# First MLP stage of the next block ahead of the second stage of this one: retention and an exact-GELU MLP on one core

## The chip, the cores and the metric

The kernel runs on one core of one Trainium2 chip. The metric is the device time of one execution in microseconds. The kernel before takes 281.17 us, the median of three runs (280.98 to 282.06).

## The reference

```python
# q, k, v: (8, 8, 576, 64) float32     batch, heads, sequence, head width
scores = (1 / sqrt(64)) * q @ k.T
gamma  = 1 - 2 ** (-5 - arange(8))               # one per head
Dmat   = where(rel >= 0, gamma ** rel, 0)        # rel = row - column
ret    = (scores * Dmat) @ v                     # retention, no softmax
x      = ret.transpose(0, 2, 1, 3).reshape(4608, 512)
h      = x @ w_in                                # (512, 2048)
g      = 0.5 * h * (1 + erf(h / sqrt(2)))        # exact GELU
out    = g @ w_out                               # (2048, 512), float32
```

## The kernel before

The 4608 tokens are cut into nine blocks of 512 (t = 0 to 8). A block goes through three parts.

**Retention** makes the transposed block xT (512 features on partitions in four chunks, 512 tokens). It works on units of 128 tokens: q, k and v are loaded with a cast to bf16 by GpSimd's DMA queue (L522, the 64-token tails of a sequence L518) into a ring of N_LD buffer pairs (qk_ld, v_ld), a pair of units to a buffer. The first ten units are transposed by TensorE (qk_ps, copied to qkT), later ones by DMA transposes that SyncE issues (L613). Then come the scores (sc), the masked scores (ret, VectorE), the scaled values (vh, VectorE L826 or eight pieces on ScalarE L829), the product of the two and of the running state (o_ps), the state itself (u_ps, copied to u_sb), and the scaling into xT (VectorE L860, L848). The rings of vh, ret and qkT have N_VH, N_RET and N_QKT buffers. The matmuls of retention come in bursts between MLP products; a burst can carry the last products of one group of units and the scores of the next together, and the numbers in APART name the groups whose scores stand by themselves.

**The first stage** multiplies xT by w_in and applies GELU, which gives g. Blocks 0 and 1 do it plainly (hT, ScalarE L1104). From block 2 on the hidden features are cut into four parts, kp = 0 to 3, and a part is done either plainly (four tiles of hT, 16 matmuls of 512 columns) or as a "unit" of seven products instead of eight quarter products (four matmuls of 256 columns each, into PSUM tiles yT, zT and xT_, in the order of PRODUCTS). A unit needs sums of xT (xs, VectorE L1059), sums of w_in (wi_sum) and a chain behind each product: copies m3 ('q') and raw ('t') of yT on VectorE or ScalarE (L573, L575), then on VectorE less (L1196), more (L1200), dif (L1209) and c11 (L1226), and four GELUs on ScalarE (L1217). LAYOUTS says for each block which parts are units, which are plain ("p") and which are woven.

**The second stage** multiplies g by w_out. Block 0 does it plainly; from block 1 on it is seven products of 16 matmuls of 256 columns for each half of rows (oT, in the order of SECOND), with sums of g (s, g, VectorE L1004) and of w_out, and with chains on ScalarE and VectorE (L1235, L1238, L1243, L1248, L1254) into o_sb, two tiles with one buffer each, that SyncE stores (L1306).

The order of all instructions is made when the kernel is built, by a planner in the kernel: each step is added with an engine, a duration, its dependencies and a due time (add), and a loop places the step that can start first, with ties broken by due times. For TensorE the MLP products come from `stream`, a list of runs: before, the first stage of block t and the second stage of block t, for t = 0 to 8. pe_candidates looks at the first LOOK products of the foremost run that still has some (for blocks 0 and 1 also of later runs). Each engine then executes its list in order and waits at semaphores. The same holds for the DMA queues: ORDER is the list of the loads up to unit 10 and of the weights (k2 is k of unit 2, wi4 the fifth eighth of w_in, L528, wo0 the first of w_out, L531), and GpSimd issues them in that order; SyncE's list has the transposes and the stores.

g has one buffer for each half of the parts (tags g0 and g1), so that a block's first stage can write g when the second stage of the block ahead has read it.

Of the kernel before, what the change touches and what calls it, by code (L numbers as in the profile page):

```python
# [9 lines left out]
FP32 = mybir.dt.float32  # L10
BF16 = mybir.dt.bfloat16
# [96 lines left out]
def kernel(  # L108
# [12 lines left out]
    B, H, S, D = q.shape  # L121
# [8 lines left out]
    TOK = 512  # L130
    HALF = TOK // 2
    N_BLK = n_tok // TOK
# [16 lines left out]
    kept = pair_of[1, 0]  # L149
# [11 lines left out]
    def slot_of(i):  # L161
# [4 lines left out]
    v_order[n:n] = kept  # L166

    N_PE_TR = 10
    N_LD = 4
    N_QKT = 4  # L170
    N_VH = 5
    N_RET = 3
    N_Q = 4
    VH_ACT = [6, 8, 10, 11, 12, 13, 14, 15, 16, 17, 19, 21, 22, 24, 27, 28, 31, 34, 35, 37]
    HOT = 10.1
    N_WARM = 8
    SLACK = 0.2
    CUTS = (0, 128, 256, 384, 512)
    AHEAD = 6
    WIDE = [2, 6, 14, 10, 4]  # L180
    VH_DUE = 14.0
    PARTS = 4
    FAST = 1
    FETCH = 4.0
    BUSY_FETCH = 6.2
    GAP_A = 0.0
    GAP_B = 1.3
    SHIFT = {4: -1.5, 5: -11.5, 6: 1.0, 7: 3.0, 8: 4.0, 9: -1.5, 10: 1.0, 11: 1.0, 12: 1.5, 13: -3.0, 14: -1.0, 15: -0.5, 16: -5.0, 17: -4.5, 18: -1.5, 19: 3.5, 20: 6.5}
    APART = [6, 7, 12]
    BEFORE = 6.1  # L190
    UNIT_FROM = 2
    LOOK = 16
    HOLD = 5.6
    LAYOUTS = {2: ['10', '2', 'p3'], 3: ['01', '2', 'p3'], 4: ['1', '02', 'p3'], 5: ['01', '2', 'p3'], 6: ['01', '23'], 7: ['01', '23'], 8: ['10', '3p2']}
    LEAD = 8.9
    SPREAD = 7.7
    EASE = 6.8
    ORDER = ("k2 wi4 q1 q2 k3 pos k1 wi0 q3 v1 v3 v2 wi3 wi6 wi1 wi7 v4 q4 wi5 k5 wi2 k4 q5 v5 wo0 wo4 wo1 wo5 q9 "
             "k7 k6 wo6 q6 q8 v10 q7 wo2 v6 wo7 v9 wo3 k10 q10 v7 k8 k9 v8").split()
    K_ORDER = [0, 1, 8, 9, 2, 3, 10, 11, 4, 5, 12, 13, 6, 7, 14, 15]  # L200
    PRODUCTS = "3251647"
    SECOND = "1267543"
    LAYOUT = {t: ["p0", "p1", "p2", "p3"] for t in range(2, N_BLK)}
    for t in range(UNIT_FROM, N_BLK):
# [2 lines left out]
    const = ctx.enter_context(tc.tile_pool(name="const", bufs=1))  # L207
    ld_pool = ctx.enter_context(tc.tile_pool(name="ld", bufs=N_LD))
    tr_pool = ctx.enter_context(tc.tile_pool(name="tr", bufs=N_QKT))
    f_pool = ctx.enter_context(tc.tile_pool(name="fold", bufs=2))  # L210
# [4 lines left out]
    g_pool = ctx.enter_context(tc.tile_pool(name="g", bufs=1))  # L215
# [4 lines left out]
    P = Plan()  # L220
# [57 lines left out]

    ld_ring, tr_ring, vh_ring, ret_ring, x_ring = Ring(N_LD), Ring(N_QKT), Ring(N_VH), Ring(N_RET), Ring(3)
    o_ring = [Ring(1), Ring(1)]  # L280
    g_ring = [Ring(1) for _ in range(2)]
    s_ring = [Ring(1) for _ in range(2)]
    f_ring, m_ring, xs_ring = Ring(2), Ring(N_Q), Ring(1)

# [1 line left out]
    def laid(t, block):  # L286


        def plain_of(kp):
            return [("1", t, m, 1, 0, TOK) for m in (2 * kp, 2 * kp + 1, 2 * kp + 8, 2 * kp + 9)]  # L290

        def unit_of(kp):
            return [("u", t, kp, p) for p in PRODUCTS]

        if block[0] == "p":
            return plain_of(int(block[1]))
        one = unit_of(int(block[0]))
        if len(block) == 1:
            return one
        if block[1] == "p":  # L300
            four = plain_of(int(block[2]))
            return [one[0], four[0], one[1], one[2], four[1], one[3], four[2], one[4], one[5], four[3], one[6]]
        return [x for two in zip(one, unit_of(int(block[1]))) for x in two]

    stream = []
    for t in range(N_BLK):
        if t < 2:
            cuts = CUTS if t == 0 else (0, 256, 512)
            for lo, hi in zip(cuts, cuts[1:]):
                stream.append([("1", t, m, 2, lo, hi) for m in K_ORDER[::2] if t or m not in WIDE])  # L310
            if t == 0:
                stream.append([("1", t, m + n, 1, 0, TOK) for m in WIDE for n in range(2)])
        else:
            stream.append([one for block in LAYOUT[t] for one in laid(t, block)])
        if t < FAST:
            stream.append([("2", t, ts, m, m + 2) for m in range(0, N_DF, 2) for ts in range(2)])
            stream.append([("2", t, ts, m, m + 4) for ts in range(2, 4) for m in range(0, N_DF, 4)])
        else:
            stream.append([("2", t, p, r, n, part) for n, p in enumerate(SECOND) for r in ((0, 1), (1, 0))[t == N_BLK - 1]
                           for part in range(2)])  # L320

    def piece_time(one):
        if one[0] == "u":
# [20 lines left out]
    first = {}  # L344
    for nm, src, eng, tag in (("q", q, nc.sync, "t"), ("k", k, nc.scalar, "t"), ("v", v, nc.sync, "o0")):
        t = first[nm] = (o_pool if nm == "v" else f_pool).tile([128, H, D], FP32, tag=tag, name=f"{nm}32")
# [7 lines left out]
    lgT = const.tile([128, HP, 1], FP32, name="lgT")  # L354
    step = const.tile([128, HP, 1], FP32, name="step")
    back_step = const.tile([128, HP, 1], FP32, name="back_step")
    val = const.tile([128, 1, 128], FP32, name="val")
    pos = const.tile([128, 1, NCI], FP32, name="pos")
    far = const.tile([128, 1, 128], FP32, name="far")
    ident = const.tile([128, 1, 128], BF16, name="ident")  # L360
    near = const.tile([128, HP, 2, 128], FP32, name="near")
    msk = const.tile([128, 1, 128], FP32, name="msk")
# [113 lines left out]

    loaded, slots, w_in_sb, w_out_sb = {}, {}, {}, {}
    touched = {}

    def tiles_of(i):  # L480

        if i not in loaded:
            n = slot_of(i)
            if i in kept:
                loaded[i] = (const.tile([128, 2, H, D], BF16, name=f"qk_ld{i}"), const.tile([128, H, D], BF16, name=f"v_ld{i}"))
                return loaded[i]
            if n not in slots:
                ld_ring.take()
                slots[n] = (ld_pool.tile([128, 2, H, 2, D], BF16, tag="qk", name="qk_ld"),
                            ld_pool.tile([128, 2, H, D], BF16, tag="v", name="v_ld"))  # L490
            qk, v_ld = slots[n]
            j = units[i][2] or 0
            if i in old:
                loaded[i] = (qk.rearrange("p a (j h) b d -> p j a (h b) d", j=2)[:, j], v_ld[:, j])
            else:
                loaded[i] = (qk[:, :, :, j], v_ld[:, j])
        return loaded[i]
# [45 lines left out]
    for item in ORDER:  # L543
        what = item.rstrip("0123456789")
        i = int(item[len(what):] or 0)
# [334 lines left out]
    for i in range(N_U):  # L880
        bp, ci, j = units[i]
# [4 lines left out]
        if i < N_PE_TR:  # L886
            for jj, nm in enumerate("qk"):
# [3 lines left out]
                    lambda engine, i=i, jj=jj: turned_copy(i, jj, engine), due - 1.0)  # L891
# [3 lines left out]
        if i not in fine and i not in tails:  # L895
# [8 lines left out]
            if ci:  # L904
# [4 lines left out]
                at=lambda i=i: 0.0 if i // 4 in x_tiles else x_ring.at())  # L909
# [16 lines left out]
        else:  # L926
            add(f"mask{n}.1", "dve", 0.6, (last if n in ALONE else [f"odd_{n}"]) + ["msk"], lambda n=n: masked(n, 1), due + 2.0,
                at=ret_ring.at)
# [4 lines left out]
    for i in v_order:  # L933
# [4 lines left out]
        if i in VH_ACT:  # L938
            step_ = H // PARTS
            for p in range(PARTS):  # L940
                name = f"vh{i}" if p == PARTS - 1 else f"vh{i}.{p}"
# [33 lines left out]
    g_tiles, s_tiles, w_sums, fold = {}, {}, {}, {}  # L975
# [9 lines left out]
    def g_of(t, m):  # L985
        kp = m % 8 // 2
        two = kp // 2
        if (t, two) not in g_tiles:
            if t:
                g_ring[two].take()  # L990
            g_tiles[t, two] = g_pool.tile([128, 2, 2, 2, TOK], BF16, tag=f"g{two}" if t else f"first{two}", name="g")
        return g_tiles[t, two][:, kp % 2]

    def g_sum(t, two, which):
# [327 lines left out]
    for run in stream:  # L1322
        for one in run:
            nm = f"mlp{one}"
            if one[0] == "1":
                _, t, m0, n, lo, hi = one
# [210 lines left out]
    def begun(one):  # L1537
# [7 lines left out]
            return one[2] in "12" or (one[2] in OPENS and one[3] == rs[0]) or BANK2[one[2]] in chain.get(("2", one[1], rs), ())  # L1545
        return True

    def pe_candidates():
        got = []
        for op in P.open["pe"]:  # L1550
            if op.name in in_macro or op.name.startswith("mlp"):
                continue
            got.append((max(T["pe"], op.ready, nth_free(op.banks)), 0, op.due, op))
        window = 0
        hold = False
        if macros and not got:
            ahead = next((W[r[0]] for r in heads if r), NEVER)
            n, ops, due = macros[0]
            hold = ahead >= due + HOLD and (macro_start(ops, False) or NEVER) <= T["pe"] + 0.3
        for run in heads:  # L1560
            if not run:
                continue
            if run[0][1] < 2:
                look = run[:1]
            else:
                look = run[:LOOK]
            for one in look:
                op = P.ops[f"mlp{one}"]
                if not op.waits and not (hold and op.banks) and begun(one):
                    got.append((max(T["pe"], op.ready, nth_free(op.banks)), 2, W[one], op))  # L1570
            window += 1
            if window >= (AHEAD if run[0][1] < 2 else 1):
                break
        got = [g for g in got if g[0] < NEVER / 2]
        if macros and not any(g[1] == 0 for g in got):
            n, ops, due = macros[0]
            at = macro_start(ops)
            if at is not None:
                at = max(at, stretch_end[0] + (GAP_B if ops[0].startswith("in_b") else GAP_A))
                ahead = next((W[r[0]] for r in heads if r), NEVER)  # L1580
                mlp = min((g[0] for g in got if g[1] == 2), default=NEVER)
                if ahead >= due or mlp > T["pe"] + 0.4:
                    got.append((at, 1, due, ops))
        if not got:
            return None
        first = min(g[0] for g in got)
        return min((g for g in got if g[0] <= first + 0.05), key=lambda g: (g[1], g[2], g[0]))
# [76 lines left out]
```

## Time and profile before

| what | value |
|---|---|
| median of three runs | 281.17 us (280.98 to 282.06) |
| the profiled execution | 281.36 us, its span 279.5 us |
| TensorE busy (PE) | 271.7 us, 97% of the span |
| VectorE busy (DVE) | 229.8 us, 82% |
| ScalarE busy (ACT) | 176.2 us, 63% |
| GpSimd busy (POOL) | 110.2 us, 39%, nearly all DMA issues |
| granted TensorE clock | 1.00 |
| units of seven products in the first stages | 23 of 28 parts |
| last matmul group ends | at 276.3 us |

PE is the matmul side of TensorE and PEld its weight loads, which overlap with it. Busy time says how long an engine had an instruction under way. The profile's waits say for whom an engine sat idle. A place in the text such as "at 121.7" is microseconds from the start of the span.

### The profile page before, as it was taken

Reading aid. Unit: us, or ns where it says so; the run is one execution under the profiler, and the core shown is the slowest. Engines: PE = TensorE matmul, PEld = TensorE weight load, DVE = VectorE, ACT = ScalarE, POOL = GpSimd, SP = SyncE. Lnnn points to the kernel's source line nnn. Section 1 sums busy time; section 2 is a strip of 40 time slices with the busy share of each in tenths; the row PEclk is TensorE's granted clock in tenths of the full one; section 3 lists DMA queues with packets and bytes.
Section 4 is the critical chain, followed back from the end, with each engine's and each line's share of the span. In section 5 each row is a group of like instructions: output and inputs, shape, how many; then the busy total and the mean of one; then the engine's idle time right before and its main releaser. Section 6 shows DMA issues by size and latency. Waiting matters only on the chain.

```text
span 279.5 us, 8688 instructions
## 1 busy us (share of the span) xinstructions
PE 271.7 (97%) x3607; PEld 215.7 (77%) x3623; DVE 229.8 (82%) x440; ACT 176.2 (63%) x434; POOL 110.2 (39%) x139
## 2 busy tenths in 40 slices
PE   7899999999999999999999999999999999999995
PEld 2584566578888688858886888778888888888784
DVE  5950757499999997899989999988799989958841
ACT  7586425567839974795189625982695379618741
POOL 8967869847546067710526448305000000000000
PEclk9999999999999999999999999999999999999999
DMA  9999999999999999999999999999700040013013
GB/s 154 165 187 172 191 169 178 136 231 144 131 131 138 214 114 142 145 198 166 130 220 115 118 139 243 145 112 94 196 2 2 6 150 4 2 38 115 0 40 113
DMA packets 152374, 35.55 MB, mean 127 GB/s; under 512 B 141072, under 2 KB 148240, under 8 KB 152336
## 3 DMA queue, kind: packets, MB, share of 16 engines
q0 software_dynamic: 115792, 17.97, 101.3%
q1 hardware_dynamic: 34912, 16.26, 34.3%
q10 hardware_dynamic: 1632, 0.79, 1.1%
q8 instruction: 28, 0.46, 0.7%
q14 instruction: 10, 0.08, 0.1%
HBM read 36.70 MB, written 9.44 MB: 165 GB/s over the span
## 4 chain that ended last, share of the span: by engine, by line
PE 78%; DMA 11%; POOL 7%; issue 1%; ACT 1%; DVE 0%; POOLq 0%; ACTq 0%
PE oT L231 37%; PE zT L231 11%; PE hT L231 8%; PE yT L231 7%; DMA qk_ld<-in_k_dram 5%; PE o_ps L231 4%; DMA qk_ld<-in_q_dram 3%; DMA w_in<-in_moe_w_in_dram 3%; POOL qk_ld L522 3%; PE sc L231 2%; PE u_ps L231 2%; POOL v_ld L522 2%; POOL qk_ld L518 1%; POOL w_in L528 1%; ACT g L1217 0%
## 5 line engine op out<-in xcount | busy, mean ns | idle before, releaser
L231 PEld LDWEIGHTS <-g 128*128 128x128 bf16 x576 | 55.0, 98 | 13.1 <-DVE g L1004 0.3
L231 PEld LDWEIGHTS <-w_in 128*128 128x128 bf16 x528 | 47.2, 98 | 15.8 <-issue 0.2
L231 PEld LDWEIGHTS <-wi_sum 128*128 128x128 bf16 x460 | 44.6, 98 | 7.8 <-issue 0.9
L231 PE MATMUL hT<-xT,w_in 128*128 128x256 bf16 (+2 forms) x334 | 49.7, 292 | 0.6
L1104 ACT ACTIVATE g<-hT 128x512 bf16<-128x512 f32 (+1 forms) x58 | 32.1, 555 | 23.4 <-PE hT L231 22.6
L231 PE MATMUL oT<-w_out,g 128*128 128x256 bf16 (+1 forms) x315 | 45.4, 293 | 0.3 <-issue 0.2
L829 ACT ACTIVATE vh<-v_ld,dv 128x64 bf16<-128x64 bf16 x152 | 41.8, 345 | 1.4 <-DVE qkT L573 1.3
L1248 ACT COPY o_sb<-oT 128x512 f32<-128x512 f32 (+1 forms) x27 | 14.5, 539 | 42.2 <-PE oT L231 35.2
L231 PEld LDWEIGHTS <-s 128*128 128x128 bf16 x384 | 37.1, 98 | 4.7
L522 POOL DMA_DIRECT2D qk_ld<-in_q_dram x31 | 27.7, 896 | 31.5 <-DMA qkT<-qk_ld 23.7
L522 POOL DMA_DIRECT2D v_ld<-in_v_dram x31 | 27.9, 903 | 14.6 <-issue 5.0
L231 PE MATMUL oT<-w_sum,s 128*128 128x256 bf16 x256 | 31.8, 273 | 0.0
L231 PE MATMUL oT<-w_sum,g 128*128 128x256 bf16 x256 | 31.3, 273 | 0.0
L522 POOL DMA_DIRECT2D qk_ld<-in_k_dram x31 | 28.0, 903 | 5.8 <-DMA v_ld<-in_v_dram 5.2
L1217 ACT ACTIVATE g<-zT 128x512 bf16<-128x512 f32 x46 | 26.2, 605 | 2.2 <-PE zT L231 1.5
L657 DVE TENSOR_TENSOR ret<-sc,msk 128x512 bf16<-128x512 f32 x36 | 23.1, 680 | 0.5 <-PE sc L231 0.5
L860 DVE TENSOR_TENSOR xT<-o_ps,dqT 128x512 bf16<-128x512 f32 x26 | 16.7, 680 | 0.6 <-PE o_ps L231 0.6
L826 DVE TENSOR_TENSOR vh<-v_ld,dv 128x512 bf16<-128x512 bf16 x17 | 11.5, 683 | 6.6 <-DMA v_ld<-in_v_dram 6.6
L573 DVE COPY qkT<-qk_ps 128x512 bf16<-128x512 bf16 x17 | 6.7, 420 | 12.3 <-PE qk_ps L235 12.3
L1196 DVE TENSOR_TENSOR q<-q,zT 128x512 f32<-128x512 f32 x23 | 14.9, 681 | 2.1 <-PE zT L231 1.9
L1254 DVE TENSOR_TENSOR o_sb<-o_sb,oT 128x512 f32<-128x512 f32 (+1 forms) x18 | 11.2, 622 | 6.4 <-PE oT L231 4.0
L1226 DVE TENSOR_TENSOR zT<-q,zT 128x512 f32<-128x512 f32 x23 | 15.6, 690 | 1.0 <-PE zT L231 0.6
(174 smaller groups left out, 461.2 us busy)
## 6 DMA issues: line engine op xcount, KB each, us to landing
out_dram<-o_sb SPq DMA_DIRECT2D x29, 256.0 KB, 3.4
qk_ld<-in_k_dram POOLq DMA_DIRECT2D x31, 128.0 KB, 8.0
qk_ld<-in_q_dram POOLq DMA_DIRECT2D x31, 128.0 KB, 8.0
v_ld<-in_v_dram POOLq DMA_DIRECT2D x31, 128.0 KB, 7.6
w_in<-in_moe_w_in_dram POOLq DMA_DIRECT2D x8, 256.0 KB, 8.0
w_out<-in_moe_w_out_dram POOLq DMA_DIRECT2D x8, 256.0 KB, 7.9
out_dram<-o_sb SPq DMA_DIRECT2D x9, 128.0 KB, 2.4
v_ld<-in_v_dram POOLq DMA_DIRECT2D x8, 64.0 KB, 6.3
```

The lines of the kernel that those rows point to most:

```text
L231: return nc.tensor.matmul(*args, **more)
L522: nc.gpsimd.dma_start(dst, src[2 * bp + j, :, ci * C:ci * C + C, :].rearrange("h s d -> s h d"))
L657: nc.vector.tensor_tensor(r, t, by, op=ALU.mult)
L826: nc.vector.tensor_tensor(vh, loaded[i][1], dv[:, :, ci:ci + 1].to_broadcast([128, H, D]), op=ALU.mult)
L829: nc.scalar.activation(vh[:, h], loaded[i][1][:, h], AF.Copy, scale=dv[:, h, ci:ci + 1])
L860: nc.vector.tensor_tensor(dst, o, dqT[:, :, ci * C:ci * C + C], op=ALU.mult)
L1104: nc.scalar.activation(g_of(t, m0)[:, m0 % 2:m0 % 2 + n, m0 // 8, lo:hi], hT, AF.Gelu)
L1196: nc.vector.tensor_tensor(q_, q_, chain[key]["Z"][1], op=ALU.subtract)
L1217: nc.scalar.activation(target(key, what), chain[key][n][1], AF.Gelu)
L1226: nc.vector.tensor_tensor(to, chain[key]["q"], z, op=ALU.add)
L1248: nc.scalar.copy(target(key, what), chain[key][n][1])
L1254: nc.vector.tensor_tensor(to, to, chain[key][n][1], op=ALU.add)
```

## The change

The order of the runs in `stream` changes. With LAG = 4 the first stage of block 4 comes right behind that of block 3, and from there on the first stage of a block stands ahead of the second stage of the block before: F3, F4, S3, F5, S4, F6, S5, F7, S6, F8, S7, S8. So g of two blocks is alive: blocks 2, 4, 6 and 8 get buffers of their own (tag "again"). Space for them comes from smaller rings (load buffers 4 to 3, vh 5 to 4, ret 3 to 2) and from sharing: the loads of the units in `kept` lie in the first "again" buffer, and two start-up tiles in a q tile. When 13 products or fewer of the foremost run are left (EDGE), TensorE may also take products of the next run. The planner's numbers are searched anew: the order of loads, the layouts, which units have their vh on ScalarE (20 before, 17 after), due times and gaps.

```diff
-    N_LD = 4
+    N_LD = 3
-    N_VH = 5
-    N_RET = 3
+    N_VH = 4
+    N_RET = 2
-    VH_ACT = [6, 8, 10, 11, 12, 13, 14, 15, 16, 17, 19, 21, 22, 24, 27, 28, 31, 34, 35, 37]
+    VH_ACT = [4, 6, 7, 8, 9, 13, 14, 16, 18, 19, 22, 24, 28, 30, 31, 32, 36]
+    EDGE = 13
-    WIDE = [2, 6, 14, 10, 4]
+    WIDE = [2, 10, 14, 12, 4]
...
-    APART = [6, 7, 12]
-    BEFORE = 6.1
+    APART = [6, 7, 8, 9, 10, 11]
+    BEFORE = 9.9
-    LOOK = 16
-    HOLD = 5.6
-    LAYOUTS = {2: ['10', '2', 'p3'], 3: ['01', '2', 'p3'], 4: ['1', '02', 'p3'], 5: ['01', '2', 'p3'], 6: ['01', '23'], 7: ['01', '23'], 8: ['10', '3p2']}
+    LAG = 4
+    LOOK = 11
+    HOLD = 6
+    LAYOUTS = {2: ['0', '12', 'p3'], 3: ['01', '2', 'p3'], 4: ['3', '2', '0p1'], 5: ['10', '23'], 6: ['01', '2p3'], 7: ['01', '23'], 8: ['01', '2', '3']}
-    ORDER = ("k2 wi4 q1 q2 k3 pos k1 wi0 q3 v1 v3 v2 wi3 wi6 wi1 wi7 v4 q4 wi5 k5 wi2 k4 q5 v5 wo0 wo4 wo1 wo5 q9 "
-             "k7 k6 wo6 q6 q8 v10 q7 wo2 v6 wo7 v9 wo3 k10 q10 v7 k8 k9 v8").split()
+    ORDER = ("k2 k1 pos q1 wi0 q3 k3 q2 v1 v2 v3 wi4 wi7 wi1 wi5 v4 k4 q5 wi6 k5 wi3 wi2 q4 wo0 v5 wo4 wo1 q9 wo5 "
+             "q8 v7 wo6 v6 q7 q6 wo2 k7 v10 wo7 wo3 k6 q10 k8 v8 k10 k9 v9").split()
-    PRODUCTS = "3251647"
+    PRODUCTS = "3251467"
...
-    g_ring = [Ring(1) for _ in range(2)]
+    g_ring = [Ring(2) for _ in range(2)]
...
+    stream = []
+    for t in range(N_BLK):
+        first_stage(t)
+        if t != LAG - 1:
+            second_stage(t - (t >= LAG))
+    second_stage(N_BLK - 1)
...
-            g_tiles[t, two] = g_pool.tile([128, 2, 2, 2, TOK], BF16, tag=f"g{two}" if t else f"first{two}", name="g")
+            g_tiles[t, two] = g_pool.tile([128, 2, 2, 2, TOK], BF16, tag=f"first{two}" if not t else f"g{two}" if t % 2 else f"again{two}", name="g")
...
+    def ending(run):
+
+        return run[0][1] > 1 and len(run) <= EDGE and not any(P.ops[f"mlp{one}"].banks for one in run) and run is heads_left()[0]
...
-            if window >= (AHEAD if run[0][1] < 2 else 1):
+            if window >= (AHEAD if run[0][1] < 2 else 1) and not ending(run):
                 break
```

The other edits are the due times SHIFT, LEAD, SPREAD and EASE, the gaps GAP_A, GAP_B and SLACK, and the sharing of space.

More of the change, by code (lines that the diff above doesn't have):

```diff
@@ L168 @@
     N_PE_TR = 10
-    N_LD = 4
+    N_LD = 3
     N_QKT = 4
-    N_VH = 5
-    N_RET = 3
+    N_VH = 4
+    N_RET = 2
     N_Q = 4
-    VH_ACT = [6, 8, 10, 11, 12, 13, 14, 15, 16, 17, 19, 21, 22, 24, 27, 28, 31, 34, 35, 37]
+    VH_ACT = [4, 6, 7, 8, 9, 13, 14, 16, 18, 19, 22, 24, 28, 30, 31, 32, 36]
     HOT = 10.1
     N_WARM = 8
-    SLACK = 0.2
+    SLACK = 0.1
+    EDGE = 13
     CUTS = (0, 128, 256, 384, 512)
     AHEAD = 6
-    WIDE = [2, 6, 14, 10, 4]
+    WIDE = [2, 10, 14, 12, 4]
     VH_DUE = 14.0
@@ L185 @@
     BUSY_FETCH = 6.2
-    GAP_A = 0.0
-    GAP_B = 1.3
-    SHIFT = {4: -1.5, 5: -11.5, 6: 1.0, 7: 3.0, 8: 4.0, 9: -1.5, 10: 1.0, 11: 1.0, 12: 1.5, 13: -3.0, 14: -1.0, 15: -0.5, 16: -5.0, 17: -4.5, 18: -1.5, 19: 3.5, 20: 6.5}
-    APART = [6, 7, 12]
-    BEFORE = 6.1
-    UNIT_FROM = 2
-    LOOK = 16
-    HOLD = 5.6
-    LAYOUTS = {2: ['10', '2', 'p3'], 3: ['01', '2', 'p3'], 4: ['1', '02', 'p3'], 5: ['01', '2', 'p3'], 6: ['01', '23'], 7: ['01', '23'], 8: ['10', '3p2']}
-    LEAD = 8.9
-    SPREAD = 7.7
-    EASE = 6.8
-    ORDER = ("k2 wi4 q1 q2 k3 pos k1 wi0 q3 v1 v3 v2 wi3 wi6 wi1 wi7 v4 q4 wi5 k5 wi2 k4 q5 v5 wo0 wo4 wo1 wo5 q9 "
-             "k7 k6 wo6 q6 q8 v10 q7 wo2 v6 wo7 v9 wo3 k10 q10 v7 k8 k9 v8").split()
+    GAP_A = 1.7
+    GAP_B = 2.4
+    SHIFT = {4: 1.5, 5: 6.5, 6: 8.5, 7: 1.0, 8: 6.5, 9: 1.5, 10: 0.0, 11: -3.5, 12: -6.0, 13: -6.5, 14: -4.5, 15: -4.0, 16: -0.5, 17: 0.5, 18: -2.0, 19: -2.0, 20: 2.0}
+    APART = [6, 7, 8, 9, 10, 11]
+    BEFORE = 9.9
+    UNIT_FROM = 2
+    LAG = 4
+    LOOK = 11
+    HOLD = 6
+    LAYOUTS = {2: ['0', '12', 'p3'], 3: ['01', '2', 'p3'], 4: ['3', '2', '0p1'], 5: ['10', '23'], 6: ['01', '2p3'], 7: ['01', '23'], 8: ['01', '2', '3']}
+    LEAD = 8
+    SPREAD = 7.5
+    EASE = 4.6
+    ORDER = ("k2 k1 pos q1 wi0 q3 k3 q2 v1 v2 v3 wi4 wi7 wi1 wi5 v4 k4 q5 wi6 k5 wi3 wi2 q4 wo0 v5 wo4 wo1 q9 wo5 "
+             "q8 v7 wo6 v6 q7 q6 wo2 k7 v10 wo7 wo3 k6 q10 k8 v8 k10 k9 v9").split()
     K_ORDER = [0, 1, 8, 9, 2, 3, 10, 11, 4, 5, 12, 13, 6, 7, 14, 15]
-    PRODUCTS = "3251647"
+    PRODUCTS = "3251467"
     SECOND = "1267543"
@@ L303, in laid, with first_stage @@
         return [x for two in zip(one, unit_of(int(block[1]))) for x in two]
-    stream = []
-    for t in range(N_BLK):
+    def first_stage(t):
         if t < 2:
@@ L314, with second_stage @@
             stream.append([one for block in LAYOUT[t] for one in laid(t, block)])
+    def second_stage(t):
         if t < FAST:
@@ L356 @@
     back_step = const.tile([128, HP, 1], FP32, name="back_step")
-    val = const.tile([128, 1, 128], FP32, name="val")
+    start_up = f_pool.tile([128, 2, HALF], FP32, tag="q", name="start_up", bufs=N_Q)
+    val, far = start_up[:, 0:1, :128], start_up[:, 1:2, :128]
     pos = const.tile([128, 1, NCI], FP32, name="pos")
-    far = const.tile([128, 1, 128], FP32, name="far")
     ident = const.tile([128, 1, 128], BF16, name="ident")
@@ L478 @@
     touched = {}
+    early = []
     def tiles_of(i):
@@ L484, in tiles_of @@
             if i in kept:
-                loaded[i] = (const.tile([128, 2, H, D], BF16, name=f"qk_ld{i}"), const.tile([128, H, D], BF16, name=f"v_ld{i}"))
+                if not early:
+                    early.append(g_pool.tile([128, 2, 2, 2, TOK], BF16, tag="again0", name="qkv_ld").rearrange("p a b h s -> p (a b h s)"))
+                at = 3 * H * D * kept.index(i)
+                loaded[i] = (early[0][:, at:at + 2 * H * D].rearrange("p (j h d) -> p j h d", j=2, h=H),
+                             early[0][:, at + 2 * H * D:at + 3 * H * D].rearrange("p (h d) -> p h d", h=H))
                 return loaded[i]
@@ L1546, in begun, with heads_left @@
         return True
+    def ending(run):
+        return run[0][1] > 1 and len(run) <= EDGE and not any(P.ops[f"mlp{one}"].banks for one in run) and run is heads_left()[0]
+    def heads_left():
+        return [run for run in heads if run]
     def pe_candidates():
```

## The prediction

> **What bounds the kernel now.** I read the page's busy shares first, then the waits of PE, the windows by stage and the timeline of the first 18 us.
>
> From the page:
>
> ```profile
> span 279.5 us, 8688 instructions
> PE 271.7 (97%) x3607; PEld 215.7 (77%) x3623; DVE 229.8 (82%) x440; ACT 176.2 (63%) x434; POOL 110.2 (39%) x139
> qk_ld<-in_k_dram POOLq DMA_DIRECT2D x31, 128.0 KB, 8.0
> ```
>
> All of PE's own waits, and three windows of 28 to 30 us (columns: length, PE, PEld, DVE, ACT, POOL, then clock and DMA):
>
> ```profile
> PE warm L231 <- DVE ln_scale L352: 1.2, 1, 1.2
> PE qk_ps L235 <- DMA qk_ld<-in_q_dram: 0.9, 2, 0.6
> PE qk_ps L235 <- DMA qk_ld<-in_k_dram: 0.6, 2, 0.4
> PE zT L231 <- ACT g L1217: 0.4, 1, 0.4
> PE oT L231 <- issue: 0.2, 1, 0.2
> ...
> 140.00:168.00 28.00, 27.90 (x369) 23.19 (x370) 26.85 (x47) 18.87 (x49) 12.27 (x14) 1.00 1.62 148
> 168.00:198.00 30.00, 29.79 (x463) 24.55 (x463) 25.83 (x46) 18.95 (x47) 12.85 (x16) 1.00 1.65 144
> 198.00:226.00 28.00, 28.00 (x485) 24.19 (x484) 27.24 (x47) 17.88 (x42) 0.00 (x0) 1.00 0.16 49
> ```
>
> PE is the bound, at full granted clock, and waits for almost nothing: 3.3 us, of which 1.2 is before its first product. DVE is close behind: 27.24 of 28 us in the last window. Between the first and the second stage of a block, where the change acts, PE doesn't stop. The chain of waits ends so (start, length):
>
> ```profile
> 263.65 0.44 PE zT L231 x4
> 264.09 12.24 PE oT L231 x112
> 276.33 0.02 issue
> 276.35 0.37 ACT o_sb L1248
> ```
>
> The last zT product of block 8 gives way to 112 products of its second stage without a pause. 12.24/112 gives 0.109 us for a product of 256 columns. In the timeline eight of 512 columns go from 47.26 to 48.99: 0.216 each. With these I place events by the PE work that stands before them. From start to start of the products PE loses after 18 us about 0.53 at 41.5 and 0.55 at 53.1 (loads not landed), 0.55 at 121.7 (zT behind ACT's g) and some 0.5 in smaller pieces: 2.1 us. That is all that a better order can take out of the middle; the order of attention bursts costs more, but stays.
>
> **The change, part by part.** The sum is made against the profiled execution, 281.36 us (span 279.5 and 1.86 around it); the median of the runs, 281.17, lies 0.19 under it. A measurement of this kernel can tell about 0.5%, 1.4 us, from no change.
>
> *First stage ahead of second.* The order of the changed kernel shows that it happens: block 4's first stage follows block 3's, and the end is stage two of 7, then of 8. It covers a wait that PE doesn't have (above): 0. The end is the same 112 products and the same last store: 0.
>
> *One more block of seven products.* The groups that appear once per such block (L1196, L1200) stand 23 times; the order of the changed kernel has 24. Seven products of four matmuls replace 16 of 512 columns: 28 x 0.109 = 3.05 against 16 x 0.216 = 3.46: **-0.40**, on PE, so on the path. Its four DVE steps of 0.60 and four ACT steps go beside PE; 24 vh pieces leave ACT for three vh of DVE, and eleven copies of q and t leave DVE. By pitch (0.60 us back to back, 1.28 for two) DVE's total falls from 224 to 220.
>
> *Attention bursts.* After 18 us there are 33 before and 36 after. In the timeline a burst with all three kinds (o_ps, u_ps, sc) takes 1.71 from MLP product to MLP product, sc alone 0.67 and o_ps with u_ps 1.26, so a split costs 0.2; two joined turns and two sc of 0.44 each give most of it back. The kinds that differ sum to 5.2 before, 5.35 after: **+0.1**.
>
> *The new load order.* The rows of before:
>
> ```profile
> 16.10 0.61 PE L231 MATMUL hT<-xT,w_in 128*128 128x128 bf16 x8
> 16.64 0.41 PE L231 MATMUL o_ps<-ret,v_ld 128*64 128x128 bf16 x8
> 16.99 0.62 PE L231 MATMUL hT<-xT,w_in 128*128 128x128 bf16 x8
> 17.54 0.41 PE L231 MATMUL o_ps<-ret,v_ld 128*64 128x128 bf16 x8
> ...
> 10.94 3.05 POOL L528 DMA_DIRECT2D w_in<-in_moe_w_in_dram  x4
> ```
>
> w_in4 was the second load of POOL's queue (issued 2.36, landed 5.8 later) and is now the eleventh, behind nine of 128 KB and w_in0. Loads land one behind the other: the first at 7.3 (1.34 + 5.9), the eleventh at 16.5 (10.08 + 6.4), 0.92 each. So the tenth, the last v, lands at 15.6, 0.9 sooner than now. The weight behind it: the early w_in0 landed 1.07 after the load ahead of it, the weight issued at 10.94 (8.1 to landing, 19.0) 2.5 after; so w_in4 lands between 16.7 and 18.1. PE comes to it after the second w_in0 products and one o_ps, with 4.4 us of work done besides the warm-up; before has 4.4 at 16.4 and 5.5 at 17.89, from where it runs on. Lag 0.2 to 1.6; neither row is nearer, I take **+0.9**. The other weights then land 0.7 us or more ahead of their products. The lag is given back: the turns at 41.5 and 53.1 wait for the load stream, and up to that of k9 both orders carry the same loads but one v, so a PE that is 0.9 late doesn't wait there: **-1.08**.
>
> [...]
>
> *Block 4 right behind block 3.* Between the starts of those first stages PE has 13.7 us of products (26.6 to 27.5 between blocks elsewhere), and DVE 15.6 us of steps up to xs of block 4. From the q copy of block 3's second unit, which can start 1.1 us into the stage, to the first xs there are 21 DVE steps, 12.4 us: xs is ready 13.6 after the stage began, PE (two bursts, 0.5 over their products) needs it at 14.2. It holds by about 0.5. In block 4 itself the less and dif steps stand behind four more xs and two vh: there PE waits some 0.2 to 0.4 at the products '6' and '4' of its first two units: **+0.3**.
>
> *The 0.55 at 121.7* came from one unit alone amid plain blocks in block 4, whose layout is gone: **-0.45**, since block 6 now has such a unit.
>
> *Three load buffers for four, four vh for five, two ret for three, two g:* the buffers are taken from the tail units first, which free early, so that the loads of a pair wait for the transposes of a tail (SP) to land. The tightest: the tail's six loads start when the state of the pair ahead is done, at 68 us of PE work; the next pair's scores come at 99. That is 31 us of work, 32 with its bursts. The chain takes 2 (q and k issued) + 4 to 7 (landing) + 3 to 10 (transpose) + 3.5 + 4 to 7 + 3 to 8: 20 to 37, likely 27. Cost 0, with 5 us of cover.
>
> *Output buffers at the end:* stage two of 8 writes into o_sb right behind stage two of 7. The c11 copy waits for a store: product 3 done, copy 0.6, issue 0.9, landing 3.4: 4.9; the product that needs the copies queued behind it comes 7 us after. Cost 0, cover 1 to 2 us.
>
> Sum: -0.40 + 0.1 + 0.9 - 1.08 + 0.3 - 0.45 = -0.63. 281.36 - 0.63 - 0.19 = **280.5 us** as a median: no change that counts.
>
> **Rivals.**
> 1. *Waits vanish altogether.* w_in4 lands as early weights did (+0.2) and the new order has no waits in PE's stream where before has 2.1: -0.40 + 0.1 + 0.2 - 2.1 = -2.2, 279.0. For it: DVE has 4 us less to do and two stages to spread it over. Against: one late release at L1217 in the middle of before shows that a planned order doesn't remove all. If even the smaller losses of bursts go, 278.5. The start alone without its lag, as if loads landed in no queue, gives 280.5 - 0.9 = 279.6; as all of the first ten loads landed 0.92 apart, it has 0.04 of the chance.
> 2. *Slower: the load ring.* If transposes land 10.5 us after issue, as one at 88.68 did, and loads after 7, the chain above takes 34 to 37 us: PE stands before block 3's first scores for 2 to 4 us, and less at the pair behind the next tail, whose chain has 30 us for 21 to 29. It decides from 32 us on. 281.2 + 2.3 = 283.5, up to 285. Against: with few loads under way transposes landed after 3.1 (194.70) and 5.7 (134.30). [...]
> 3. *Slower: DVE ends last in blocks 3 and 4.* If its steps there go at their length, 0.68, and not at the pitch of 0.60, the 21 steps take 1.7 more: 1.2 late for block 4, and the 22 steps of block 4 1.0 more: 281.2 - 0.6 + 2.2 = 282.8. Against: the timeline has 0.60 from step to step even in the chain of a unit.
>
> **How the numbers follow.** Forecast 0.49 (279.8 to 282.5, the ends of the lag and of block 4's waits); rival 1 0.28, the 0.04 of a start without lag among it; rivals 2 and 3 together 0.23, ring a little more than DVE. Chances: faster 0.28, same 0.49, slower 0.23. The range goes from 278.8 (most of rival 1) to 283.4 (rival 3 and the near half of rival 2).
>
> **What would show it.** Matmuls in the groups of zT and xT grow by a 24th; first w_in4 product between 16.7 and 18.1, and no wait of qk_ps for DMA at 41 and 53; no wait of PE at the first products of block 4 (near 127 us); no wait of sc or PEld for qkT by DMA near 114. The forecast is wrong if PE shows waits of over 1 us in the middle, for DMA (rival 2) or DVE (rival 3), or if PE's span without waits moves by more than 0.5.

## The result and the profile after

The changed kernel takes **310.16 us** (median of six executions, 308.85 to 312.44) against 281.36 us for the kernel before on the same chip: a ratio of 1.1023, 95% interval 1.0985 to 1.1061. It is 28.8 us slower, where the prediction was 280.5 us, no change that counts.

The page of the changed kernel's profiled execution (310.82 us), the rows that answer to those shown of before, and the strips of 40 slices for TensorE (PE) and its granted clock:

```profile
span 308.7 us, 8743 instructions
PE 281.2 (91%) x3633; PEld 220.8 (72%) x3633; DVE 224.9 (73%) x432; ACT 177.4 (57%) x427; POOL 110.5 (36%) x139
PE   7999999999899993999999991999909999999995
PEclk9999999999999998999999997799966999999999
qk_ld<-in_k_dram POOLq DMA_DIRECT2D x29, 128.0 KB, 6.4
```

DVE and ACT are not busier than before (229.8 and 176.2 us there). PE has 9.5 us more under way, in part because its products run at half speed for a while (below). PE's strip has holes at three places, and the clock's strip has an 8, two 7 and two 6 there. The same in windows (columns: length, PE, PEld, DVE, ACT, POOL, clock, DMA share, GB/s):

```profile
100.00:120.00 20.00, 15.90 (x288) 13.56 (x285) 15.34 (x29) 10.05 (x36) 14.02 (x16) 1.00 1.87 112
120.00:140.00 20.00, 19.37 (x198) 15.05 (x199) 17.21 (x31) 14.38 (x28) 5.26 (x6) 0.91 1.93 178
180.00:200.00 20.00, 13.25 (x257) 10.62 (x256) 8.51 (x16) 5.81 (x17) 1.27 (x2) 0.83 0.95 127
220.00:240.00 20.00, 12.09 (x194) 9.13 (x193) 3.92 (x7) 4.78 (x14) 3.16 (x5) 0.74 0.55 87
```

PE's own waits (in all, times, longest), in place of the 3.3 us of before:

```profile
PE u_ps L233 <- ACT vh L844: 8.2, 3, 7.7
PE u_ps L233 <- ACT o_sb L1253: 6.5, 1, 6.5
PE sc L233 <- DMA qkT<-qk_ld: 5.5, 2, 4.7
```

From start to start of its products PE stands for 4.89 us at 115.6, 6.67 at 184.9 and 7.88 at 223.1. Over all bursts of attention work, from MLP product to MLP product, that and some smaller waits make 55.9 us where before has 31.6: 24.3 more. After each of the three the MLP products run at half speed for a while (0.21 us from one of 256 columns to the next, for 0.109); 44 products lose about 0.1 us each that way, 4.4 us in all. Together that is 28.7 of the 29.5 us between the two profiled executions.

**The first stop** is in the chain of waits (start, length, what); the chain of before has no DMA after 53.5 us:

```profile
107.72 1.63 DMA qk_ld<-in_q_dram
109.35 11.23 DMA qkT<-qk_ld
120.63 0.77 PE sc L233 x32
```

The scores of the first pair of units of a new pair of sequences (units 18 and 19, behind the tail unit 17) wait for its transposes. The first row names the profile's inferred releaser; by their landings the transpose waited for k of unit 19 (below). GpSimd's timeline tells why the transposes are late (the brackets give the idle time before and what ended it):

```profile
82.23 1.38 POOL L533 DMA_DIRECT2D qk_ld<-in_q_dram  x2 [8.92 <-PE u_ps L233]
...
96.71 0.89 POOL L537 DMA_DIRECT2D qk_ld<-in_q_dram  x1 [10.38 <-DMA qkT<-qk_ld]
97.59 0.89 POOL L537 DMA_DIRECT2D qk_ld<-in_k_dram  x1
101.65 0.88 POOL L537 DMA_DIRECT2D v_ld<-in_v_dram  x1 [3.17 <-ACT vh L844]
102.52 0.88 POOL L537 DMA_DIRECT2D qk_ld<-in_q_dram  x1
103.38 0.90 POOL L537 DMA_DIRECT2D qk_ld<-in_k_dram  x1
```

The tail's six loads (L533) get their buffer when a pair's state products (u_ps) are done. The next pair's loads (L537) get that of the tail when the tail's transposes have landed, and its v waits 3.2 us more for the vh that reads the old contents of that buffer. Its last k, issued at 103.38, lands at 108.57; the transpose issued behind it lands 11.2 us later.

**The second and third stops** have a longer chain. Of SyncE's list (rows of its sequencer), of ScalarE's, and of the chain again:

```profile
154.44 27.55 SPq L628 DMA_TRANSPOSE qkT<-qk_ld  x6
182.09 2.01 SPq L1321 DMA_DIRECT2D out_dram<-o_sb  x4
```

```profile
181.72 0.57 ACT L844 ACTIVATE vh<-v_ld,dv 128x64 bf16<-128x64 bf16 x2
191.30 0.37 ACT L1253 COPY o_sb<-oT 128x256 f32<-128x256 f32 x1 [9.01 <-DMA out_dram<-o_sb]
191.57 0.59 ACT L844 ACTIVATE vh<-v_ld,dv 128x64 bf16<-128x64 bf16 x2
```

```profile
183.65 7.55 DMA out_dram<-o_sb
```

The stores of block 3 stand in SyncE's list behind transposes that wait for late loads. Its sequencer is at these transposes from 154.44 to 181.99, so the stores are issued from 182.09 and landed at 191.2. Each half of a block has one o_sb, so ScalarE's c11 copy of the next second stage (L1253) waits 9.0 us for the store, the vh pieces behind it in ScalarE's list wait too, and PE's u_ps products wait for vh. ScalarE's waits for a store, of before and of the changed kernel:

```profile
ACT o_sb L1238 <- DMA out_dram<-o_sb: 0.9, 1, 0.9
```

```profile
ACT o_sb L1253 <- DMA out_dram<-o_sb: 19.4, 2, 10.4
```

At 223 it is the same once more: loads of the last tail at 219.04, transposes at 222.88, stores from 225.62 to a landing at 230.2.

### The profile page after: what moved, and what is told of

Its sections match the earlier page's. It is cut to its first block, busy times and chain, and to the rows that moved or that the text cites. A ratio compares the mean times of both kernels' runs of the same rounds, so it can differ in the third digit from the quotient of the medians.

```text
span 308.7 us, 8743 instructions
## 1 busy us (share of the span) xinstructions
PE 281.2 (91%) x3633; PEld 220.8 (72%) x3633; DVE 224.9 (73%) x432; ACT 177.4 (57%) x427; POOL 110.5 (36%) x139
## 4 chain that ended last, share of the span: by engine, by line
PE 61%; DMA 20%; POOL 9%; SPq 3%; issue 3%; ACT 2%; DVE 0%; POOLq 0%; ACTq 0%
PE oT L233 24%; PE hT L233 11%; DMA qkT<-qk_ld 9%; PE zT L233 8%; PE yT L233 5%; DMA qk_ld<-in_k_dram 5%; POOL qk_ld L537 4%; DMA out_dram<-o_sb 3%; POOL v_ld L537 2%; PE o_ps L233 2%; SPq L628 2%; DMA qkv_ld<-in_q_dram 2%; PE sc L233 2%; PE u_ps L233 1%; POOL qk_ld L533 1%
## 5 line engine op out<-in xcount | busy, mean ns | idle before, releaser
L233 PEld LDWEIGHTS <-wi_sum 128*128 128x128 bf16 x480 | 47.4, 99 | 8.9 <-issue 0.7
L537 POOL DMA_DIRECT2D qk_ld<-in_q_dram x29 | 26.6, 918 | 61.1 <-PE u_ps L233 36.6
L233 PE MATMUL hT<-xT,w_in 128*128 128x256 bf16 (+2 forms) x328 | 45.6, 291 | 0.0
L1119 ACT ACTIVATE g<-hT 128x512 bf16<-128x512 f32 (+1 forms) x54 | 29.7, 557 | 10.8 <-PE hT L233 10.2
L844 ACT ACTIVATE vh<-v_ld,dv 128x64 bf16<-128x64 bf16 x128 | 35.3, 348 | 1.0 <-DMA v_ld<-in_v_dram 1.0
L233 PE MATMUL oT<-w_sum,s 128*128 128x256 bf16 x256 | 33.4, 281 | 0.0
L1232 ACT ACTIVATE g<-zT 128x512 bf16<-128x512 f32 x48 | 28.0, 615 | 1.2 <-DVE zT L1241 0.8
L537 POOL DMA_DIRECT2D v_ld<-in_v_dram x29 | 26.8, 923 | 4.6 <-ACT vh L844 3.2
L537 POOL DMA_DIRECT2D qk_ld<-in_k_dram x29 | 26.8, 924 | 1.3 <-issue 0.8
L233 PE MATMUL u_ps<-vh,qk_ld 128*64 128x64 bf16 (+1 forms) x304 | 11.1, 199 | 14.7 <-ACT vh L844 8.2
L533 POOL DMA_DIRECT2D qk_ld<-in_q_dram x8 | 5.5, 694 | 40.6 <-PE u_ps L233 40.0
L233 PE MATMUL sc<-qkT 64*64 64x128 bf16 (+2 forms) x544 | 14.9, 214 | 5.7 <-DMA qkT<-qk_ld 5.5
L1253 ACT COPY o_sb<-oT 128x256 f32<-128x256 f32 x16 | 5.8, 372 | 23.5 <-DMA out_dram<-o_sb 19.4
L1269 DVE TENSOR_TENSOR o_sb<-o_sb,oT 128x512 f32<-128x512 f32 (+1 forms) x18 | 11.2, 625 | 11.2 <-PE oT L233 11.1
```

What stands on the lines that cost most here:

```text
L233: return nc.tensor.matmul(*args, **more)
L533: nc.gpsimd.dma_start(dst, src[2 * bp + jj, :, ci * C:S, :].rearrange("h s d -> s h d"))
L537: nc.gpsimd.dma_start(dst, src[2 * bp + j, :, ci * C:ci * C + C, :].rearrange("h s d -> s h d"))
L844: nc.scalar.activation(vh[:, h], loaded[i][1][:, h], AF.Copy, scale=dv[:, h, ci:ci + 1])
L1119: nc.scalar.activation(g_of(t, m0)[:, m0 % 2:m0 % 2 + n, m0 // 8, lo:hi], hT, AF.Gelu)
L1232: nc.scalar.activation(target(key, what), chain[key][n][1], AF.Gelu)
```

## Experiments

Theory A: the ring of three load buffers makes loads and transposes late, and all three stops follow from that. Theory B: it is the stores behind transposes on SyncE's queue, with one o_sb for each half. Theory C: the new order of the stages crowds ScalarE and VectorE, whatever the buffers. The ratio behind each time is to the kernel before, run on the same chip as that experiment.

**e1: four load buffers again**, order of all engines as in the changed kernel.

```diff
-    ld_pool = ctx.enter_context(tc.tile_pool(name="ld", bufs=N_LD))
+    ld_pool = ctx.enter_context(tc.tile_pool(name="ld", bufs=4))
```

> The changed kernel with four load buffers again and every engine's order of instructions kept: only the number of buffers behind the loads differs. To make the room, the decay factors of all chunks share one tile, so the output is not the reference's. Theory A (load buffers): with a ring of three, GpSimd's loads wait for u_ps products, the transposes come late, and all three long TensorE stalls (115.6, 184.9, 223.1 us) follow from that: with four buffers all three go and the time is 281 to 286. Theory B (stores behind transposes on SyncE's queue, one o_sb for each half): the stall at 115.6 goes, the two at 185 and 223 become shorter only as far as the transposes come earlier: 285 to 300. Theory C (the new order itself crowds ScalarE and VectorE, whatever the buffers): 305 to 312.

Measured: 282.87 us, ratio to before 1.0062 (1.0038 to 1.0086). The strips of this run, and the only wait of PE over 0.4 us once its products run:

```profile
PE   7999999999998999999999999999999999999995
PEclk9999999999999999999999999999999999999999
```

```profile
PE sc L233 <- DMA qkT<-qk_ld: 1.0, 1, 1.0
```

One buffer takes back 27.3 of the 28.8 us. The tail's loads are issued from 75.70 and those of the next pair from 83.97, where the changed kernel has 82.23 and 96.71. So C is out, and B is out as a cause of its own: with loads on time the stores behind the transposes cost nothing. The shared decay factors are not what helps: e5 below has them too and keeps the first stop, and e10 does without them. What is left is a wait of 1.2 us (start to start) for one transpose at 85.5.

**e2: stores issued by ScalarE.**

```diff
-    def store(t, half, ..., queue=nc.sync):
+    def store(t, half, ..., queue=nc.scalar):
```

> The changed kernel with the stores of blocks 0 to 7 issued by ScalarE instead of SyncE, at the place in the order at which they were planned; three load buffers as in the changed kernel. Theory A with its second link (late transposes hold up the stores on SyncE's queue, so ScalarE's copy waits for o_sb): the stall at 115.6 us stays (4.9 us and the half clock behind it), the stalls at 185 and 223 (6.7 and 7.9 us and the half clock behind them) shrink below 2 us: 288 to 296, some of it ScalarE's time for issuing. If the loads alone make all three stalls, without the stores: 303 to 312. Theory C: 305 to 312.

Measured: 308.86 us (1.0984; 1.0904 to 1.1063), a miss for A's price. The two u_ps stops are gone, and the first stays with 3.7 us, as A has it. But new ones come: 6.3 us at 122.4, 3.7 at 186.2 in front of scores. ScalarE's timeline shows the first:

```profile
118.87 8.72 ACTq L1321 DMA_DIRECT2D out_dram<-o_sb  x2
127.64 0.59 ACT L590 COPY t<-yT 128x512 f32<-128x512 f32 x1 [10.87 <-DMA qkT<-qk_ld]
```

The second of these two stores is issued at 127.25; it counts on the same semaphore (118) as the transpose issued at 115.14, eight DMAs of SyncE and ScalarE back in the program's order, which lands at 127.23. So here a store on another queue still waits for a late transpose, and ScalarE is idle for 10.87 us before its next copy. This run doesn't price the link by itself; e5 does.

**e3: the kernel before with three load buffers**, order kept (bufs=3 in the same line).

> The kernel before with three load buffers instead of four, every engine's order of instructions kept. Theory A: the smaller ring alone makes loads and transposes late: TensorE stalls of several us at scores from 100 us on, 288 to 312. Theory C (it is the new order): 281 to 283, no stall over 1 us.

Measured: 297.87 us (1.0607; 1.0573 to 1.0640). Waits of PE and of ScalarE:

```profile
PE sc L231 <- ACT o_sb L1238: 12.1, 2, 6.2
```

```profile
ACT o_sb L1238 <- DMA out_dram<-o_sb: 19.0, 3, 8.8
```

The ring alone costs the old kernel 16.7 us, through the same link of store, o_sb and ScalarE, at 158.5 and 224.2. The stop at 115 isn't there in the old order.

**e4: the changed kernel without the new order.**

```diff
-    LAG = 4
+    LAG = 99          # every second stage right behind its first
```

> The changed kernel with its buffers and all its searched numbers, but with the second stage of every block directly behind its first one, as in the kernel before; the plan is made anew with that. Theory A: late loads as in the changed kernel, 288 to 312. Theory C: no long stall, 280 to 286.

Measured: 303.41 us (1.0798; 1.0761 to 1.0834), stops of 4.7 us at 163.4 and 7.5 at 228.1, as A expected.

**e5: two o_sb for each half**, three load buffers.

```diff
-    o_pool = ctx.enter_context(tc.tile_pool(name="o", bufs=1))
+    o_pool = ctx.enter_context(tc.tile_pool(name="o", bufs=2))
```

> The changed kernel with two output buffers for each half of a block instead of one, three load buffers and every engine's order as in the changed kernel. To make the room, the decay factors of all chunks share one tile and the two heads of a pair share their factors, so the output is not the reference's. Theory A with its second link (transposes that wait for late loads hold up the stores behind them on SyncE's queue; ScalarE's copy then waits for the one o_sb and u_ps for ScalarE): the stall at 115.6 us stays at 4 to 5 us, those at 185 and 223 shrink below 2 us, or to what the late transposes by themselves still cost a few us later, and the time is 290 to 300. Without that link, all three from the loads directly: 305 to 312.

Measured: 296.25 us (1.0512; 1.0459 to 1.0566). PE's waits:

```profile
PE sc L233 <- DMA qkT<-qk_ld: 10.0, 3, 5.2
```

Both u_ps stops are gone. The first stop stays (5.4 us, as loads and transposes are as late as in the changed kernel), and at 186.2 late transposes now hold up scores for 3.4 us directly; at 223 no wait for a transpose is left. So the link through o_sb and ScalarE is worth 13.9 of the 28.8 us (310.16 less 296.25), and what is left, 14.8 us over the kernel before, is mostly the late transposes in front of scores; four buffers still left 1.7 (e1).

**e6: the planner's count mended.** The planner puts products on PE by its own books. When it runs, the buffers of units 4 and 5 are given back three times: `read` gives a buffer back at every read after the last one that is needed, and there two inner products follow the state. So it plans with two load buffers too many, five for three (six for four in the kernel before).

```diff
-        if i not in kept and want <= got:
+        if i not in kept and want <= got and n not in given:
+            given.add(n)
             ld_ring.give(...)
```

> The changed kernel, three load buffers, with one error of its planner mended: the buffers of the pair of units 4 and 5 are given back three times in its books (once at the state, twice more at the inner products), so that it plans with two more load buffers than there are, five for three (six for four in the kernel before). Now each is given back once, and the plan is made anew. Theory A with a plan that knows the ring: scores and states are put later on TensorE, behind other products; the stalls shrink, but three buffers are too few for the loads even so: 288 to 303. If the error in the books is the whole cause: 280 to 285. If the ring has nothing to do with it: 305 to 315.

Measured: 294.74 us (1.0458; 1.0406 to 1.0511). With books that know of three buffers the long stops become many short ones (the largest 3.3 us at 192.6), and 13.3 us are still lost to before: three buffers are too few for pairs and tails together, and the wrong count made it 15.4 worse.

**e7: without the new order, with four load buffers** (the edits of e4 and e1).

> As the experiment without the new order (second stage of every block directly behind its first), with four load buffers behind the same plan; the decay factors of all chunks share one tile, so the output is not the reference's. It gives, beside the changed kernel with four buffers (282.87), what the new order is worth where the ring does not stall. Theory A: all stalls over 2 us go, 281 to 286; and if the new order brings nothing, within 0.5% of 282.87. Theory C (the new order costs time of its own): 1.5 us or more below 282.87.

Measured: 287.15 us (1.0213; 1.0159 to 1.0268), a little over what A expected, and one stop of 2.1 us stays, at 81.3. With four buffers the new order is 4.3 us faster than the old one under the same numbers; with three it is 6.8 slower (310.16 against 303.41). C, by which the order costs time, is the wrong way round here. The searched numbers belong to the new order, so 4.3 is what the order brings under them, not under numbers of its own.

**e8: four buffers in pools and plan, count mended**, dqT and near in bf16 for the room.

> The changed kernel with four load buffers, counted rightly by its planner (each given back once), the plan made anew; the room comes from keeping the decay factors (dqT, near) in bf16. If the remaining wait of 1.2 us at 85.5 us in the run with four buffers comes from the wrong count, it goes: 280 to 282, equal to the kernel before or up to 0.5% faster. If the new order itself leaves waits whatever the plan knows: 282 to 285.

Measured: 284.14 us (1.0082; 1.0047 to 1.0117). The wait at 85.5 went, no wait over 0.8 us is left in the profile, and the time didn't fall. The first of the two expectations is wrong; the second names no cause, and the runs give none.

**e9: a load buffer of its own for the tails**, three for the pairs.

```diff
-  slots[n] = (ld_pool.tile([...], tag="qk", ...), ld_pool.tile([...], tag="v", ...))
+  own = dict(bufs=1) if n in tails else {}
+  slots[n] = (ld_pool.tile([...], tag="qkt" if own else "qk", ..., **own), ...)   # v alike
```

> The changed kernel with the ring of three left to the pairs of units and one load buffer of its own for the four tails (the same memory as four buffers), every engine's order kept; the decay factors of all chunks share one tile, so the output is not the reference's. It asks which part of the ring makes the loss. If the tails in the ring do (the tail's loads wait for the pair ahead, and the next pair's for the tail), all three long stalls go, as with four buffers: 282 to 288. If three buffers are too few for the pairs by themselves: stalls stay at one or two of the three places, 290 to 305. Theory C: 305 to 312.

Measured: 282.71 us (1.0045; 1.0027 to 1.0062). GpSimd's longest wait:

```profile
POOL qk_ld L538 <- PE u_ps L233: 62.5, 9, 18.0
```

PE has no stop over 1.7 us, and the granted clock is 1.00. GpSimd still waits 62.5 us for u_ps, where the changed kernel has 76.6 (40.0 at L533 and 36.6 at L537), but the 22.6 us that GpSimd waits there for transposes are gone, and the loads come in time for PE. Three buffers are enough for the pairs; the tails among them make the loss.

**e10: four buffers in pools and plan**, books as they were, dqT and near in bf16 as in e8, and **e11: the same with one us more for every landing** (`SAFE = 2.5` for 1.5).

> The changed kernel with four load buffers in the pools and in the plan, the room taken from the decay factors kept in bf16; the planner's books are left as they are. If the 282.87 of the run with four buffers and shared decay factors stands for the ring alone: 281.5 to 284. If the wait of 1.2 us at 85.5 us goes with the new plan: 280.5 to 282.

> As the run before this one, and the planner counts every landing of a DMA after 55 us one us later (2.5 instead of 1.5 us of margin), so that scores are put later behind the transposes. If late transposes are what is left: no wait over 0.6 us, 280.5 to 282. If the later scores only push the second stages back: 283 to 285.

Measured: 282.15 us (1.0038; 1.0022 to 1.0053) and 283.60 us (1.0083; 1.0066 to 1.0100). e10 leaves nothing of the reference out and is the best form of the change, 0.4% behind the kernel before. More room costs more than it saves, and leaves waits of 1.1 us at 52.8 and 1.2 at 91.5. None of the versions beats the kernel before.

**e12: all three rings at their former sizes** (ld 4, vh 5, ret 3), order kept.

> The changed kernel with all three rings at their former sizes (four load buffers, five vh, three ret), every engine's order kept; the decay factors of all chunks share one tile and the two heads of a pair share their factors, so the output is not the reference's. If the rings of vh and ret cost something beside the load ring: 280 to 282, clearly below the 282.87 with four load buffers alone. If they cost nothing, as the prediction had it: 282 to 284.

Measured: 282.73 us (1.0050; 1.0032 to 1.0068), the same as e1. With four load buffers the smaller rings of vh and ret cost nothing.

## Why the prediction was wrong

- **The step that failed** is "Three load buffers for four, four vh for five, two ret for three, two g: ... Cost 0, with 5 us of cover". e1 and e12 put 27.3 us on the load ring and nothing on vh and ret. The place was right: the tail's loads that wait for a state, the transposes of the tail, the next pair's loads. e9 shows that the tails in the ring are what costs. The size was off: the term of the last transpose and the time to the last load were too small. The chain, "20 to 37, likely 27", took 38.4 us (82.23 to 120.6) in a slot of 33.5 (to 115.7). Its terms, as they came: six loads issued over 4.1 and landed by 90.8, a sum of 8.5 (2 for the issue of q and k and 4 to 7 expected); tail transposes landed at 96.16, 5.4 later (3 to 10); 7.2 until the last k is issued (3.5; the wait of 3.2 for vh was in no term); its landing 5.2 (4 to 7), 0.8 to the next issue, and 11.2 for the last transpose (3 to 8). Only two terms lie above their ranges, 7.2 for 3.5 and 11.2 for at most 8; inside them the chain would have taken 31.5 and fitted the slot. The trace of before could have told the second: half of its 30 transposes land more than 8 us after issue, the slowest 11.3 (issued 74.26). The terms at their upper ends add up to 37.5, and I took 27 as likely.
- **Rival 2 was the right mechanism at its first place, with a wrong price.** It had "2 to 4 us" there and less at the next tail: 283.5, up to 285. The first stop is 4.9 us. What was missing is the second link: SyncE's transposes wait for loads, stores wait behind transposes, o_sb waits for stores, ScalarE's list waits for o_sb, PE for vh. I priced o_sb only at the end of the kernel ("Cost 0, cover 1 to 2 us"), where no transposes are left. By e5 that link is worth 13.9 us. The half clock behind the stops, 4.4 us in all, was in no price.
- *First stage ahead of second: 0.* Not refuted. With four buffers e7 has the order 4.3 us ahead of the old one, but under numbers that were searched for the new one; what it is worth by itself is open.
- *Rival 3 (DVE last in blocks 3 and 4) and theory C* are out: with e1 no wait over 0.4 us is left after 88 us.
- *The start, +0.9:* wrong. PE runs on from 17.82 (17.89 before); w_in4, issued 10.27, landed at 16.5, below the 16.7 of the bound. *Turn waits, -1.08:* half. The one at 41.5 is gone, that at 53 is 0.75 in the changed kernel and 0.55 in e1. *The 0.55 at 121.7* went from that place, as said. *Block 4, +0.3:* not there: in e1 no loss in block 4's first stage (127.7 to 141.5) is over 0.06 us. In its place came 0.28 at 149.6, in block 3's second stage, and 0.36 at 163.3, in block 5's first (zT behind ACT's g again), which were in no term.
- *The rest of the sum.* It gave 0.6 us below before; e1, e9, e10 and e12, without the ring's cost, are 0.8 to 1.7 above, e8 2.7. In e1 and e9 a wait of 1.2 and 1.7 us at 85.5 and 80.7 fills that; in e8 (at most 0.8) and e10 there is no such wait, and PE's first MLP product is later (14.01 against 13.35 before). In the profiled executions of e10 and of before that later start is all of the difference: from the first MLP product to the last e10 takes 262.3 us, before 262.7. What else keeps e8 above is open. The gain of 0.40 by the 24th unit can't be read: a few matmul records are missing in the trace of before, and one of 512 columns is 0.22.

## What to carry to other kernels

A chain that is priced as "20 to 37 against 32" has no cover: price it at its upper end, with the queue's worst landings in the trace, before calling it 0. When a buffer ring shrinks, follow the late transfer past the engine that first waits: list what stands behind it in the list of every engine and queue, and whose buffer that frees. And when a change of order and a change of buffers come together, keep the order and put the buffer back: here the number of load buffers alone told 27 us apart from the rest.

## What the runs showed of the hardware

- The granted clock was 0.50 at or behind each of the three stops of the changed kernel: from 121.00 to 124.42, from 189.27 to 196.10 and from 226.82 to 237.06, where the stops begin at 115.6, 184.9 and 223.1. These are 3.41, 6.83 and 10.24 us by the trace's clock records, one, two and three times 3.413. The windows shown lack 0.09, 0.17 and 0.26 of the clock over 20 us, which at half clock is 3.6, 6.8 and 10.4 us. The length of the stop alone does not decide it: in e7's profiled execution a stop of 2.1 us inside an attention burst was followed by 3.4 us at half clock (granted 0.96, 0.50 and 0.68 in windows of 2 us from 82 to 88), while one of 1.7 in e9 left the clock at 1.00, and with one of 3.7 in e2 (115.0 to 118.8) it kept 90% or more in the slice from 114.3 to 122.0. What else counted is shown by no run.
- A transpose of SyncE landed 2.6 us after issue with two loads still under way (before, 196.50) and 2.8 with two (the changed kernel, 224.33), but 11.2 with six under way at its issue and seven more issued before it landed (the changed kernel, 109.35), and 11.3 with seven under way (177.27). The loads beside the one at 109.35 are as slow: the four issued from 109.46 to 112.06 took 9.8 to 11.9 us, where the median of the k loads is 6.4. What makes both slow together is shown by no run.
- In e2 a DMA issued by ScalarE waited for one of SyncE: a store and a transpose count on the same semaphore, and the store is issued at 127.25, when the transpose has landed at 127.23.
